# First feed-forward layer: VectorE's operands moved to PSUM, GpSimd's work kept to SBUF

## The chip, the cores and the metric

One core of one Trainium2 chip runs the whole program. The metric is the device time of one execution in microseconds (us). TensorE (PE) multiplies matrices out of SBUF into PSUM; VectorE (DVE), ScalarE (ACT) and GpSimd (POOL) do the elementwise work; SyncE (SP) issues the DMAs. In this program POOL takes operands from SBUF alone; DVE and ACT read SBUF and PSUM.

## The reference

Causal block attention, then two feed-forward layers over the 2304 tokens, with 512 model and 2048 hidden columns. The first layer is the one that the change touches:

```
x = attention(q, k, v)                       # 4 batches, 8 heads, 576 positions, 64 per head
h = x @ w_in                                 # layer 1
g = h * clip(h + 3, 0, 6) / 6
x = g @ w_out
h = x @ w_in2                                # layer 2
g = h * tanh(softplus(h))
out = g @ w_out2
```

Everything is float32, and the kernel keeps that precision by splitting each factor of a product into a high part (rounded to PE's fp32r format) and a low part (the value minus its high part), and adding three products: high by high, high by low, low by high.

## The kernel before

**Stages.** Attention fills the first 205 us of the profiled execution, layer 1 runs to about 575 us, layer 2 to the end. Layer 1 works on five blocks of tokens, four of 512 and one of 256. For each block j and each of 16 slices f of 128 hidden columns there is one step n = 16 j + f: `in1(n)` (12 matmuls, 4 pieces of the model columns by 3 products) puts h into one of two PSUM banks, `h0` and `h1` in turn; `activate1(n)` makes g from it; `out1(n)` (12 matmuls) adds g @ w_out into the four PSUM banks `y0` to `y3`. PE's order is written out in `sequence()`: in1(n), out1(n-2), in1(n+1), out1(n-1), and so on. So in1(n+2), which writes the bank of in1(n) again, begins three sets of 12 matmuls after in1(n) has ended. After a block's last step the four y banks are copied out (`o`) by ACT or DVE, and the next block's first out1 writes them again.

**One step's elementwise work** (`activate1`): ACT writes e = relu(h + 3); DVE writes e = min(e, 6) * h, which is 6 g (L985); ACT writes its high part gh; POOL subtracts, gl = e - gh (L873). Buffers e, gh and gl have three copies each.

**Weights of layer 1** arrive as raw 64-bit words, as two halves c of 512 columns (c = 0 is w_in's, c = 1 w_out's). `rebase` turns a half into float32 in four instructions: ACT writes the scaled high word to a PSUM bank, `r0` or `r1`; POOL writes the sign to an SBUF buffer (`val` or `q`, in turn by f); DVE ORs the shifted low word into that buffer (L895: two SBUF operands); DVE ORs the shifted PSUM bank into it (L899). Then ACT writes the high part `wh` (L922), and POOL, or for c = 1 POOL or DVE, the low part `wl` (L925). `first_weights` does that for f = 4 to 15 while block 0 runs; the earlier ones are made during attention and are not touched.

**Weights of layer 2** are prepared in layer 1 too, by 16 calls of `unit2`, from block 1 on: each rebases two halves, makes four sums `S` of 256 columns, high parts (`hx`, `Sh`, by ACT) and low parts, and stores all to HBM (`w2d`). The two rebased halves go to `q` and `val`, one pair of buffers for even units and one for odd units.

**Tokens** of blocks 1 to 4 (`tokens1`): loads of two halves and a scale, an add on POOL, a multiply by the scale on DVE (L1003), high part on ACT, low part (`xl`, `X`) on DVE or POOL.

**What sets the order.** `Schedule` takes these operations with their dependences, engines and costs, runs a list scheduler over them and issues them in that order, so every engine's queue is fixed when the program is built. Where an operation may run on either of two engines (`either`), it chooses. Kinds in `SHARED` (DVE with SBUF operands alone, POOL) are counted as slower while the other engine works; the kind DVE_PSUM is not. A DMA is counted as landing 2.5 us after its issue.

## Time and profile before

| | |
|---|---|
| median of 3 runs (lowest to highest) | 971.47 us (971.42 to 972.88) |
| profiled execution: its own time / its span | 971.55 us / 969.8 us |
| PE, DVE, ACT, POOL busy, share of the span | 97%, 71%, 54%, 70% |

The span goes from the first to the last instruction of the trace. The profiled execution's own time is 1.75 us longer than its span and 0.08 us above the median. Matmuls overlap one another, so that "97% busy" counts a waiting PE as busy in part. How far PE runs at its full pace is better read from how many matmuls a stretch holds.

### The profile page before, as it was taken

What the parts mean: (1) busy time and instruction counts of PE and PEld (TensorE: products, weight loads), DVE (VectorE), ACT (ScalarE), POOL (GpSimd) and SP (SyncE); (2) the same over time, 40 slices, a digit from 0 to 9 for tenths busy, and PEclk for the clock granted to TensorE, in tenths of its full rate; (3) what the DMA queues carried; (4) which work ended last, traced back from release to release, by engine and by line L of the source; (5) the groups of instructions that cost most, each with busy time, mean ns of one, the idle gap of its engine ahead of it and who ended that gap; (6) DMA issues with size and microseconds to landing.
All of it is one profiled execution on the core that took longest, in us unless ns stands there. A gap on an engine that the chain in (4) does not pass through costs nothing.

```text
span 969.8 us, 16014 instructions
## 1 busy us (share of the span) xinstructions
PE 942.8 (97%) x5300; PEld 857.6 (88%) x5300; DVE 687.8 (71%) x1125; ACT 524.7 (54%) x1241; POOL 678.4 (70%) x663
## 2 busy tenths in 40 slices
PE   8999999999999999999999999999999999999998
PEld 6888889878777877788778899999999999999998
DVE  6798887889899777967841125466689766886567
ACT  4888888865555355445522244554464554744443
POOL 7455554569999789968842237477788877967775
PEclk9999999999999999999999999999999999999999
DMA  5777776799138988788830015867779877787752
GB/s 166 186 198 199 199 180 181 230 297 390 58 99 256 300 272 281 264 283 291 283 123 1 0 45 184 282 237 263 260 242 339 292 252 265 260 293 272 260 192 102
DMA packets 131427, 212.87 MB, mean 220 GB/s; under 512 B 45841, under 2 KB 72465, under 8 KB 131345
## 3 DMA queue, kind: packets, MB, share of 16 engines
q1 hardware_dynamic: 131344, 211.86, 66.8%
q8 instruction: 41, 0.67, 0.3%
q14 instruction: 42, 0.34, 0.1%
HBM read 154.66 MB, written 48.31 MB: 209 GB/s over the span
## 4 chain that ended last, share of the span: by engine, by line
PE 49%; DVE 2%; POOL 2%; DMA 1%; issue 1%; SPq 0%; ACT 0%; POOLq 0%; DVEq 0%
PE y L879 8%; PE y L881 8%; PE y L880 8%; PE h L881 5%; PE h L880 5%; PE h L879 5%; PE r L881 3%; PE r L880 3%; PE r L879 3%; DMA w2d<-hx 1%; POOL gl L873 1%; DMA Sh<-x2d 0%; DVE e L985 0%; DVE S L1026 0%; POOL S L1026 0%
## 5 line engine op out<-in xcount | busy, mean ns | idle before, releaser
L873 POOL TENSOR_TENSOR gl<-e,gh 128x512 fp32r<-128x512 f32 (+1 forms) x79 | 105.8, 1340 | 90.0 <-ACT gh L870 78.9
L879 PE MATMUL y<-gh,wh 128*128 128x512 f32 (+1 forms) x320 | 118.7, 371 | 4.1 <-DVE o L966 3.2
L880 PE MATMUL y<-gl,wh 128*128 128x512 f32 (+1 forms) x320 | 118.4, 370 | 0.0
L881 PE MATMUL y<-gh,wl 128*128 128x512 f32 (+1 forms) x320 | 118.4, 370 | 0.0
L985 DVE SCALAR_TENSOR_TENSOR e<-e,h 128x512 f32<-128x512 f32 (+1 forms) x78 | 48.8, 626 | 81.1 <-ACT e L870 81.1
L1185 DVE TENSOR_TENSOR sgh<-y,sgh 128x384 f32<-128x384 f32 x129 | 69.9, 554 | 32.3 <-PE y L881 32.1
L657 DVE TENSOR_TENSOR t<-t,t 128x512 fp32r<-128x512 f32 (+2 forms) x144 | 69.8, 521 | 23.8 <-ACT t L652 23.6
L870 ACT ACTIVATE gh<-e 128x512 fp32r<-128x512 f32 (+1 forms) x78 | 45.7, 586 | 70.3 <-DVE e L985 70.0
L606 ACT ACTIVATE p<-s,nm 128x64 f32<-128x64 f32 (+2 forms) x144 | 75.0, 529 | 11.9 <-DVE nm L595 11.8
L870 ACT ACTIVATE e<-h 128x512 f32<-128x512 f32 (+1 forms) x78 | 42.5, 544 | 70.4 <-PE h L881 64.1
L879 PEld LDWEIGHTS y<-gh,wh 128*128 128x128 f32 x320 | 60.5, 189 | 15.7 <-ACT o L968 2.7
L880 PEld LDWEIGHTS y<-gl,wh 128*128 128x128 f32 x320 | 60.6, 189 | 10.6 <-POOL gl L873 0.6
L881 PEld LDWEIGHTS y<-gh,wl 128*128 128x128 f32 x320 | 60.6, 189 | 10.1
L881 PE MATMUL h<-xh,wl 128*128 128x512 f32 (+1 forms) x176 | 65.6, 373 | 2.6 <-POOL wl L925 2.6
L880 PE MATMUL h<-xl,wh 128*128 128x512 f32 (+1 forms) x176 | 65.5, 372 | 2.5 <-DVE xl L873 2.5
L676 PEld LDWEIGHTS o<-t,vh 128*128 128x128 f32 x448 | 65.0, 189 | 3.1 <-ACT x L686 0.9
L646 PE MATMUL t<-ident,p 128*128 128x128 f32 x400 | 63.8, 282 | 3.2 <-DVE t L657 3.0
L595 DVE TENSOR_REDUCE nm<-s 128x1 f32<-128x64 f32 (+2 forms) x144 | 63.2, 476 | 5.1 <-PE s L575 5.1
L879 PE MATMUL h<-xh,wh 128*128 128x512 f32 (+1 forms) x176 | 65.4, 372 | 0.3 <-DVE e L985 0.3
L676 PE MATMUL o<-t,vh 128*128 128x320 f32 (+3 forms) x448 | 63.8, 282 | 0.8 <-ACT x L689 0.6
L879 PE MATMUL y<-xh,wh 128*128 128x384 f32 x192 | 64.2, 334 | 0.2 <-issue 0.2
L880 PE MATMUL y<-xl,wh 128*128 128x384 f32 x192 | 64.1, 334 | 0.0
(198 smaller groups left out, 3069.5 us busy)
## 6 DMA issues: line engine op xcount, KB each, us to landing
raw<-w SPq DMA_DIRECT2D x64, 512.0 KB
wh<-w2d SPq DMA_DIRECT2D x48, 512.0 KB
wl<-w2d SPq DMA_DIRECT2D x48, 512.0 KB
wh<-w2d SPq DMA_DIRECT2D x48, 384.0 KB
wl<-w2d SPq DMA_DIRECT2D x48, 384.0 KB
x1d<-x SPq DMA_DIRECT2D x64, 144.0 KB
qb<-qs SPq DMA_DIRECT2D x30, 288.0 KB
w2d<-Sh SPq DMA_DIRECT2D x32, 256.0 KB
```

The lines of the kernel that those rows point to most:

```text
L595: nc.vector.tensor_reduce(nm[:, c:c + 1], sc, axis=AX.X, op=ALU.max, negate=True)
L606: nc.scalar.activation(t, sc, AF.Exp, bias=nm[:, c:c + 1], accum_out=su[:, i:i + 1])
L646: nc.tensor.transpose(tp[:, c, :], t[:, o:o + P], ident)
L657: nc.vector.tensor_sub(z[:, 1, loc, :], tp, f32(z[:, 0, loc, :]))
L676: nc.tensor.matmul(out, lhsT, g[:, t, m0:m1, l, hs], start=(c == t == 0), stop=last and t == 1)
L870: lambda e: nc.scalar.activation(dst, src, func, **kw), after=after)
L873: return plan.add(engines, reads, writes, lambda e: ENG[e].tensor_sub(dst, a, b), **kw)
L879: nc.tensor.matmul(b, wh, xh, start=start and k == 0, stop=False, skip_group_check=True)
L880: nc.tensor.matmul(b, wh, xl, start=False, stop=False, skip_group_check=True)
L881: nc.tensor.matmul(b, wl, xh, start=False, stop=last, skip_group_check=True)
L985: lambda _: nc.vector.scalar_tensor_tensor(e, e, 6.0, h, op0=ALU.min, op1=ALU.mult))
L1185: nc.vector.tensor_add(place(to), bank(b), place(at))
```

## The change

- **`rebase`** now builds the value in the PSUM bank: POOL's sign goes to a scratch buffer; DVE shifts the bank and ORs the sign into it, in place (PSUM and SBUF operands); DVE then ORs the shifted low word (SBUF) with the bank, and writes to the bank itself for c = 0, or to the SBUF buffer for c = 1 (`VAL`). The count of instructions is as before.
- **`first_weights`**: the half c = 0 stays in PSUM bank r0, from which ACT makes wh and DVE (always) wl. The half c = 1 is as before, with wl on either engine.
- **`activate1`**, from block 1 on: DVE writes 6 g over h in its PSUM bank, ACT makes gh from there, and DVE, no longer POOL, makes gl. Block 0 is as before.
- **`tokens1`**: the multiply and the low part are on POOL, except for block 1, where either engine may do both.
- **`unit2`**: the first rebased half is always in r0, the second always in `val1`; there are no longer two pairs in turn. Sums that read r0 are on DVE, the one that doesn't is on POOL. The low parts of `hx` go to `q0` (DVE) and `q1` (POOL) and are stored from there; those of `S` are on POOL.

```diff
--- before.py
+++ after.py
@@ -855,6 +855,7 @@
             buf["X", n, h] = xt[0, 0, n][h] if n < KT else xp.tile(
                 [P, 512], F32R, tag=f"x{'hl'[h]}", name=f"X{n}_{h}")
+    VAL = 1
     W = lambda f, h: weight_tiles(0, f)[h]
     one = lambda e, kind, n: ((e, cost(kind, n), kind in SHARED),)
     either = lambda n: one("DVE", "DVE", n) + one("POOL", "POOL", n)
@@ -880,24 +881,28 @@
             nc.tensor.matmul(b, wh, xl, start=False, stop=False, skip_group_check=True)
             nc.tensor.matmul(b, wl, xh, start=False, stop=last, skip_group_check=True)
-    def rebase(raw, place, val, r, v):
-        high = raw[:, :, 1].bitcast(F32)
-        to, t = buf["r", place], ("r", place)
-        copy(512, [r], [t], to, high, scale=REBASE)
+    def rebase(raw, r, s, names, val=None):
+        high, low = raw[:, :, 1].bitcast(F32), raw[:, :, 0]
+        rn, t, sn, vn = names
+        ids = [len(plan.ops) + n for n in range(4)]
+        copy(512, [rn], [t], r, high, scale=REBASE)
         plan.add(
-            one("POOL", "POOL_ONE", 512), [r], [v], lambda e: nc.gpsimd.tensor_scalar(
-                val, high, 0.0, 1.0, op0=ALU.mult, op1=ALU.mult))
-        bits = val.bitcast(U32)
-        ids = [len(plan.ops) - 2, len(plan.ops) - 1]
-        ids.append(plan.add(
-            one("DVE", "DVE", 512), [r, v], [v],
+            one("POOL", "POOL_ONE", 512), [rn], [sn], lambda e: nc.gpsimd.tensor_scalar(
+                s, high, 0.0, 1.0, op0=ALU.mult, op1=ALU.mult))
+        bits = r.bitcast(U32)
+        to = bits if val is None else val.bitcast(U32)
+        plan.add(
+            one("DVE", "DVE_PSUM", 512), [t, sn], [t],
             lambda e: nc.vector.scalar_tensor_tensor(
-                bits, raw[:, :, 0], 29, bits, op0=ALU.logical_shift_right, op1=ALU.bitwise_or)))
+                bits, bits, 3, s.bitcast(U32), op0=ALU.logical_shift_left, op1=ALU.bitwise_or))
         plan.add(
-            one("DVE", "DVE_PSUM", 512), [t, v], [v],
+            one("DVE", "DVE_PSUM", 512), [rn, t], [t if val is None else vn],
             lambda e: nc.vector.scalar_tensor_tensor(
-                bits, to.bitcast(U32), 3, bits, op0=ALU.logical_shift_left, op1=ALU.bitwise_or))
+                to, low, 29, bits, op0=ALU.logical_shift_right, op1=ALU.bitwise_or))
         return ids
     def first_weights(f):
@@ -911,17 +916,17 @@
         for c in range(2) if not early else ():
             dma(512, [], [names[c]], raw[c].rearrange("p n t -> p (n t)"),
                 w1[f, :, 512 * c:512 * c + 512].bitcast(U32))
+        tag = ("val", "q")[f % 2]
         for c in range(2):
-            tag = ("val", "q")[f % 2]
-            done += rebase(raw[c], c, buf[tag, c], names[c], (tag, c))
+            done += rebase(
+                raw[c], buf["r", c], buf[tag, c], (names[c], ("r", c), (tag, c), (tag, c)),
+                buf[tag, c] if c == VAL else None)
         for c in range(2):
             cs = slice(512 * c, 512 * c + 512)
-            v = buf[tag, c]
+            v, vn = (buf[tag, c], (tag, c)) if c == VAL else (buf["r", c], ("r", c))
+            copy(512, [vn], [("wt", f, c, 0)], W(f, 0)[:, cs], v, psum=c != VAL, after=done)
             plan.add(
-                one("ACT", "ACT", 512), [(tag, c)], [("wt", f, c, 0)],
-                lambda e, cs=cs, v=v: nc.scalar.activation(W(f, 0)[:, cs], v, AF.Copy), after=done)
-            plan.add(
-                one("POOL", "POOL", 512) if c == 0 else either(512), [(tag, c), ("wt", f, c, 0)],
+                either(512) if c == VAL else one("DVE", "DVE_PSUM", 512), [vn, ("wt", f, c, 0)],
                 [("wt", f, c, 1)], lambda e, cs=cs, v=v: ENG[e].tensor_sub(
                     W(f, 1)[:, cs], v, f32(W(f, 0)[:, cs])), after=done)
@@ -979,13 +984,18 @@
         at = ("h", n % 2), ("e", n % 3), ("gh", n % 3), ("gl", n % 3)
         if "a" in parts:
             copy(w, [at[0]], [at[1]], e, h, AF.Relu, True, bias=3.0)
+        if n < FT:
+            g, gn = e, at[1]
+        else:
+            g, gn = h, at[0]
         if "c" in parts:
             plan.add(
-                one("DVE", "DVE_PSUM", w), [at[0], at[1]], [at[1]],
-                lambda _: nc.vector.scalar_tensor_tensor(e, e, 6.0, h, op0=ALU.min, op1=ALU.mult))
+                one("DVE", "DVE_PSUM", w), [at[0], at[1]], [gn],
+                lambda _: nc.vector.scalar_tensor_tensor(g, e, 6.0, h, op0=ALU.min, op1=ALU.mult))
         if "g" in parts:
-            copy(w, [at[1]], [at[2]], gh, e)
-        sub(one("POOL", "POOL", w), [at[1], at[2]], [at[3]], gl, e, f32(gh))
+            copy(w, [gn], [at[2]], gh, g, psum=n >= FT)
+        sub(one("POOL", "POOL", w) if n < FT else one("DVE", "DVE_PSUM", w), [gn, at[2]], [at[3]],
+            gl, g, f32(gh))
     def tokens1(j, k):
         t0, w = BLOCKS[j]
@@ -998,49 +1008,59 @@
                 rsd[k, h:h + 1, t0:t0 + w].to_broadcast([64, w]))
         plan.add(
             one("POOL", "POOL", w), [r, l], [r], lambda e: nc.gpsimd.tensor_add(raw, raw, low))
+        of = either(w) if j == 1 else one("POOL", "POOL", w)
         plan.add(
-            one("DVE", "DVE", w), [r, s, ("xn", 0, 0), ("xn", 0, 1)], [r],
-            lambda e: nc.vector.tensor_mul(raw, raw, rs))
+            of, [r, s, ("xn", 0, 0), ("xn", 0, 1)], [r],
+            lambda e: ENG[e].tensor_mul(raw, raw, rs))
         hi, lo = (buf["X", X(j, k), h][:, :w] for h in range(2))
         at = [("X", X(j, k), h) for h in range(2)]
         copy(w, [r], [at[0]], hi, raw)
-        sub(either(w), [r, at[0]], [at[1]], lo, raw, f32(hi))
+        sub(of, [r, at[0]], [at[1]], lo, raw, f32(hi))
     def unit2(u):
         q, c = u // 2, u % 2
-        at = [("q", u % 2), ("val", u % 2)]
+        at = [("r", 0), ("val", 1)]
         vs = [buf[x] for x in at]
         dst = w2d[q, c].rearrange("t p (s c) -> t p s c", c=256)
         for i in range(2):
             raw = buf["raw", i]
             dma(512, [], [("raw", i)], raw.rearrange("p n t -> p (n t)"),
                 w2[2 * q + i, :, 512 * c:512 * c + 512].bitcast(U32))
-            rebase(raw, i, vs[i], ("raw", i), at[i])
+            rebase(
+                raw, buf["r", i], buf["val", i], (("raw", i), ("r", i), ("val", i), ("val", i)),
+                buf["val", i] if i else None)
         cc, ch = buf["S"], buf["Sh"]
         a11, a12, a21, a22 = vs[0][:, 0:256], vs[0][:, 256:512], vs[1][:, 0:256], vs[1][:, 256:512]
-        def sums(n, a, b, reads, add=False):
+        psum = lambda n: one("DVE", "DVE_PSUM", n)
+        pool = lambda n: one("POOL", "POOL", n)
+        def sums(n, a, b, reads, of, add=False):
             plan.add(
-                either(256), reads, [("S", n)],
+                of, reads, [("S", n)],
                 lambda e: (ENG[e].tensor_add if add else ENG[e].tensor_sub)(cc[:, n], a, b))
-        sums(0, a21, a22, [at[1]], True)
-        sums(3, a11, a21, at)
-        sums(1, cc[:, 0], a11, [at[0], ("S", 0)])
-        sums(2, a12, cc[:, 1], [at[0], ("S", 1)])
+        sums(0, a21, a22, [at[1]], pool(256), True)
+        sums(3, a11, a21, at, psum(256))
+        sums(1, cc[:, 0], a11, [at[0], ("S", 0)], psum(256))
+        sums(2, a12, cc[:, 1], [at[0], ("S", 1)], psum(256))
         view = lambda t: t.rearrange("p (s c) -> p s c", c=256)
+        lo = [view(buf["q", n]) for n in range(2)]
         parts = (
-            (512, view(buf["hx", 0]), view(vs[0]), ("hx", 0), [at[0]], slice(0, 4, 3)),
-            (256, view(buf["hx", 1])[:, 0:1], view(vs[1])[:, 1:2], ("hx", 1), [at[1]], slice(6, 7)),
-            (512, ch[:, 0:2], cc[:, 0:2], ("Sh", 0), [("S", 0), ("S", 1)], slice(1, 3)),
-            (512, ch[:, 2:4], cc[:, 2:4], ("Sh", 1), [("S", 2), ("S", 3)], slice(4, 6)),
+            (512, view(buf["hx", 0]), view(vs[0]), ("hx", 0), [at[0]], slice(0, 4, 3), lo[0], [("q", 0)]),
+            (256, view(buf["hx", 1])[:, 0:1], view(vs[1])[:, 1:2], ("hx", 1), [at[1]], slice(6, 7),
+             lo[1][:, 0:1], [("q", 1)]),
+            (512, ch[:, 0:2], cc[:, 0:2], ("Sh", 0), [("S", 0), ("S", 1)], slice(1, 3), None, None),
+            (512, ch[:, 2:4], cc[:, 2:4], ("Sh", 1), [("S", 2), ("S", 3)], slice(4, 6), None, None),
         )
-        for i, (n, x, v, xn, vn, cs) in enumerate(parts):
-            copy(n, vn, [xn], x.bitcast(F32R), v)
+        for i, (n, x, v, xn, vn, cs, to, tn) in enumerate(parts):
+            of = pool(n) if i else psum(n)
+            to, tn = (v, vn) if to is None else (to, tn)
+            copy(n, vn, [xn], x.bitcast(F32R), v, psum=not i)
             dma(n // 2, [xn], [("w2d", q, c, 0, i)], dst[0][:, cs], x)
-            sub(either(n), vn + [xn], vn, v.bitcast(F32R), v, x)
-            dma(n // 2, vn, [("w2d", q, c, 1, i)], dst[1][:, cs], v)
+            sub(of, vn + [xn], tn, to.bitcast(F32R), v, x)
+            dma(n // 2, tn, [("w2d", q, c, 1, i)], dst[1][:, cs], to)
     WSLOTS = {(0, 0): (7, 8), (1, 0): (9, 10), (0, 1): (11, 12), (1, 1): (13, 14)}
```

Two places in the engines' queues show it. On DVE in block 0, between the c3 instructions (6 g) of steps 7 and 9; first before (names: `e` the activation, `h_0_2` and `h_0_3` the two h banks, `r_3255` and `r_3260` the banks r0 and r1, `raw_0` and `raw_1` the two raw halves):

```order
L985 SCALAR_TENSOR_TENSOR e_3208<-e_3208,h_0_3_3228 128x512
L925 TENSOR_TENSOR wl_8_3515<-val_3263,wh_8_3514 128x512
L895 SCALAR_TENSOR_TENSOR q_3262<-raw_1_3298,q_3262 128x512
L895 SCALAR_TENSOR_TENSOR val_3258<-raw_0_3299,val_3258 128x512
L899 SCALAR_TENSOR_TENSOR q_3262<-r_3260,q_3262 128x512
L899 SCALAR_TENSOR_TENSOR val_3258<-r_3255,val_3258 128x512
L895 SCALAR_TENSOR_TENSOR val_3263<-raw_1_3300,val_3263 128x512
L985 SCALAR_TENSOR_TENSOR e_3270<-e_3270,h_0_2_3215 128x512
```

and the same place of DVE's queue with the change:

```order
L994 SCALAR_TENSOR_TENSOR e_3208<-e_3208,h_0_3_3228 128x512
L900 SCALAR_TENSOR_TENSOR r_3260<-r_3260,val_3263 128x512
L930 TENSOR_TENSOR wl_9_3310<-r_3255,wh_9_3309 128x512
L904 SCALAR_TENSOR_TENSOR val_3263<-raw_1_3312,r_3260 128x512
L900 SCALAR_TENSOR_TENSOR r_3255<-r_3255,val_3258 128x512
L904 SCALAR_TENSOR_TENSOR r_3255<-raw_0_3311,r_3255 128x512
L994 SCALAR_TENSOR_TENSOR e_3270<-e_3270,h_0_2_3215 128x512
```

Every row between the two c3 instructions now has one operand in PSUM, and the low part made there is that of the half c = 0. On DVE in block 1, from the c3 of step 26 on (`S`, `Sh`, `hx` belong to a unit of layer 2's weights), before:

```order
L985 SCALAR_TENSOR_TENSOR e_3270<-e_3270,h_0_2_3215 128x512
L899 SCALAR_TENSOR_TENSOR q_3262<-r_3255,q_3262 128x512
L1026 TENSOR_TENSOR S<-S,q_3262 128x256
L1026 TENSOR_TENSOR S<-q_3262,S 128x256
L873 TENSOR_TENSOR S<-S,Sh 128x512
L985 SCALAR_TENSOR_TENSOR e_3193<-e_3193,h_0_3_3228 128x512
L895 SCALAR_TENSOR_TENSOR val_3258<-raw,val_3258 128x512
L899 SCALAR_TENSOR_TENSOR val_3258<-r_3260,val_3258 128x512
```

and with the change:

```order
L994 SCALAR_TENSOR_TENSOR h_0_2_3215<-e_3270,h_0_2_3215 128x512
L874 TENSOR_TENSOR gl_3272<-h_0_2_3215,gh_3271 128x512
L874 TENSOR_TENSOR q_3257<-r_3255,hx_3259 128x512
L900 SCALAR_TENSOR_TENSOR r_3260<-r_3260,val_3263 128x512
L904 SCALAR_TENSOR_TENSOR val_3263<-raw,r_3260 128x512
L994 SCALAR_TENSOR_TENSOR h_0_3_3228<-e_3193,h_0_3_3228 128x512
L900 SCALAR_TENSOR_TENSOR r_3255<-r_3255,val_3258 128x512
L904 SCALAR_TENSOR_TENSOR r_3255<-raw,r_3255 128x512
L874 TENSOR_TENSOR gl_3206<-h_0_3_3228,gh_3200 128x512
L1042 TENSOR_TENSOR S<-S,r_3255 128x256
```

The product is written over h, its low part gl has come to DVE, behind zero to two other instructions, and the subtraction S<-S,Sh has left it for POOL.

## Rows read from the trace of the kernel before

**Rows 1.** The page's busy times: us, share of the span, count of instructions.

```profile
PE 942.8 (97%) x5300; PEld 857.6 (88%) x5300; DVE 687.8 (71%) x1125; ACT 524.7 (54%) x1241; POOL 678.4 (70%) x663
```

**Rows 2.** Stretches, PE alone: from:to, us, busy (matmuls), granted clock, DMA share, GB/s.

```profile
214.34:282.00 67.66, 65.38 (x286) 1.00 0.53 196
282.00:310.00 28.00, 25.55 (x109) 1.00 0.73 235
...
355.00:388.00 33.00, 30.80 (x132) 1.00 0.81 268
388.00:406.00 18.00, 15.93 (x63) 0.91 0.85 282
...
470.00:494.00 24.00, 21.28 (x92) 1.00 0.83 284
```

**Rows 3.** Stretches, all engines: us, then PE, PEld, DVE, ACT, POOL, clock, DMA.

```profile
205.00:290.00 85.00, 82.10 (x360) 66.42 (x359) 77.11 (x83) 47.61 (x86) 80.00 (x65) 1.00 0.57 204
...
205.00:496.00 291.00, 279.27 (x1207) 225.46 (x1206) 240.60 (x274) 148.73 (x272) 250.65 (x213) 0.99 0.76 257
```

**Rows 4.** PE's waits, 205 to 500 us: total us, times, longest us.

```profile
PE y L879 <- DVE o L966: 3.2, 2, 2.1
PE h L881 <- POOL wl L925: 2.6, 3, 1.8
PE h L880 <- DVE xl L873: 2.5, 2, 1.5
PE h L879 <- DVE e L985: 2.0, 4, 0.8
```

**Rows 5.** DVE's groups by shape, 205 to 496 us: count, busy us, mean ns, idle.

```profile
L895 DVE SCALAR_TENSOR_TENSOR val<-raw,val 128x512 uint32<-128x512 uint32 x28 | 35.4, 1263 | 24.2 <-POOL val L889 24.2
L895 DVE SCALAR_TENSOR_TENSOR q<-raw,q 128x512 uint32<-128x512 uint32 x28 | 33.5, 1196 | 2.9 <-POOL q L889 2.9
L985 DVE SCALAR_TENSOR_TENSOR e<-e,h 128x512 f32<-128x512 f32 x49 | 33.1, 676 | 1.2 <-ACT e L870 1.1
L873 DVE TENSOR_TENSOR S<-S,Sh 128x512 fp32r<-128x512 f32 x20 | 23.6, 1187 | 5.4 <-ACT Sh L870 2.8 <-POOL S L1026 2.3
...
L1003 DVE TENSOR_TENSOR xr<-xr,xn 128x512 f32<-128x512 f32 x12 | 15.8, 1313 | 0.0
```

**Rows 6.** POOL's groups by shape, the same stretch and columns.

```profile
L873 POOL TENSOR_TENSOR gl<-e,gh 128x512 fp32r<-128x512 f32 x49 | 75.4, 1538 | 14.5 <-ACT gh L870 13.8 <-DVE q L895 0.5
L889 POOL TENSOR_SCALAR val<-raw 128x512 f32<-128x512 f32 x28 | 22.5, 806 | 2.8 <-DMA w2d<-val 2.0 <-POOL gl L873 0.7
```

**Rows 7.** DVE and POOL in order of time: start us, us, instruction.

```profile
269.29 1.80 DVE L895 SCALAR_TENSOR_TENSOR val<-raw,val 128x512 uint32<-128x512 uint32 x1
...
391.86 0.41 DVE L873 TENSOR_TENSOR val<-val,hx 128x256 fp32r<-128x256 f32 x1
...
270.50 1.71 POOL L925 TENSOR_TENSOR wl<-q,wh 128x512 fp32r<-128x512 f32 x1
272.18 1.28 POOL L873 TENSOR_TENSOR gl<-e,gh 128x512 fp32r<-128x512 f32 x1
```

**Rows 8.** PE in order of time: first matmul of out1(0) and of in1(4).

```profile
214.34 0.39 PE L879 MATMUL y<-gh,wh 128*128 128x512 f32 x1
...
219.78 0.39 PE L879 MATMUL h<-xh,wh 128*128 128x512 f32 x1
```

**Rows 9.** The chain of waits near 438 us: start us, us, what.

```profile
438.24 0.61 DVE e L985
438.87 0.64 ACT gh L870
439.58 0.51 POOL gl L873
```

**Rows 10.** A wait for a store, 205 to 500 us; DVE at block 4's loads.

```profile
ACT hx L870 <- DMA w2d<-hx: 14.3, 15, 4.1
...
487.51 0.43 DVE L1003 TENSOR_TENSOR xr<-xr,xn 128x256 f32<-128x256 f32 x1 [2.13 <-DMA xn<-rsd]
```

## The prediction

> **What bounds the kernel now.** Read the page's busy times first [rows 1]: PE is at 97%, so the end is set by PE's work plus what PE waits. Then ask where it waits. The pace comes from PE's order of time: out1(0) and out1(1), 24 matmuls, take 219.78 - 214.34 = 5.44 us [rows 8], 0.2267 us each, 2.72 us for a set of 12, 5.44 us for a step. A matmul's record, 0.39 us, is 1.7 times that, so a stretch of L us at full pace lists L / 0.2267 + 1.7 matmuls, those cut by its edges among them. The same sum for the slow stretches [rows 2] gives what PE lost: 214 to 282 us holds 286 of 300, 3.2 us; 282 to 310 holds 109 of 125, 3.7; 355 to 388 holds 132 of 147, 3.4; 388 to 406 holds 63 of 81, 4.1; 470 to 494 holds 92 of 107.5, 3.5. Together 17.9 us, all inside layer 1. That is the whole purse; layer 2 keeps PE full.
>
> Who made PE wait [rows 4]: copies of y out of PSUM by DVE at block ends, low parts of weights by POOL, low parts of tokens by DVE, and DVE's product e (the h bank not yet free). Four causes, two engines, so look at those as a whole: from 205 to 290 us DVE is busy 77.1 and POOL 80.0 of 85 us; over the layer 240.6 and 250.7 of 291 us [rows 3]. They are full, and their instructions are long for a reason that the groups show [rows 5]: the shift L895, with two SBUF operands, takes 1263 or 1196 ns on average, while L985, same size, with one operand in PSUM, takes 676 on average over 49 instances, beside the same POOL. In order of time it is plain on both sides [rows 7]: a shift of 1.80 us and a POOL subtraction of 1.71 us lie over each other, and the subtraction at 272.18, of the same shape, takes 1.28. So two SBUF operands on DVE cost 0.5 to 1.1 us for each instruction and 0.4 us for POOL's beside it. [...]
>
> **The change part by part**, against 971.55 us (span 969.8 plus 1.75; the median is 971.47).
>
> *DVE, 205 to 496 us.* The 56 low shifts get a PSUM operand: 35.4 + 33.5 = 68.9 us become 56 x 0.68 = 38.1, a gain of 30.8. The 20 subtractions S<-S,Sh leave: 23.6. Of 12 wide multiplies of tokens 7 leave: 7 x 1.31 = 9.2 [rows 5]. The gl of steps 16 to 49 arrive: 34 x 0.68 = 23.1 more. The other moves (sums of 256 columns, 31 to 48, at 0.41 [rows 7] instead of up to 1.1; low parts from r0 in place of those from SBUF) come out level to within about 6 us. Net -40, DVE at some 200 of 291 us.
>
> *POOL.* 34 gl leave: 34 x 1.54 = 52.3 [rows 6]. S<-S,Sh arrives: 20 x 1.28 = 25.6. The multiplies arrive: 11 of 512 columns and 4 of half that, about 17. Some 7 low parts of weights leave, 7 x 1.7 = 12 [rows 7]. Net -22, before what every remaining instruction saves where DVE no longer lies over it (up to 0.4 us). POOL at 200 to 230.
>
> *Block 0, by step.* DVE had the product, two shifts of 1.23, two ORs with r (one PSUM operand, so 0.68) and one low part of about 1.1: 5.6 us against PE's 5.44, so it fell behind until PE waited. Now 0.68 + 4 x 0.68 + 0.68 = 4.1. POOL: 1.54 + 2 x 0.81 + 1.5 x 1.7 = 5.7, now 1.28 + 2 x 0.81 + 1.28 = 4.2. Both have over 1 us of room in each step. The loop that is now serial, r0 held from ACT's write until wl is made, is an ACT write, two DVE instructions, an ACT copy and a DVE subtraction: 2 x 0.64 + 3 x 0.68 = 3.3 us plus five hand-overs, under 0.1 us each by the chain near 438 us (0.61 + 0.64 of 1.34 [rows 9]); under 4 us of the 5.44. Of the 6.9 us lost between 214 and 310 I keep 1.0 (0.5 for a step in which two chains meet, 0.5 for the block's end).
>
> *Blocks 1 to 3.* The h bank is now held for ACT's e, the product, gh and gl: about 0.65 + 1.34 + 0.68 = 2.7 us (from product to gl 1.34 [rows 9]), and PE wants it after three sets, 8.16 us; 5.5 us of cover. If that cover goes, each us beyond it is a us of PE. Of the 3.4 us between 355 and 388 I keep 0.7. At the block's end the two copies of y on DVE stood behind instructions of 1.4 to 1.8 us and now stand behind 0.7; with no wait of 2 us the clock should not fall either; of 4.1 I keep 1.0.
>
> *The end, 470 to 494 us.* The token low part (longest wait 1.5 [rows 4]) should go; the wait at the block's end has DVE behind a load, 2.13 us for the scale [rows 10], which the change doesn't touch. Of 3.5 I keep 1.8.
>
> *Queues.* SP's bytes are the same; in each unit the stores of S and Sh now stand ahead of those of hx and q, and q is stored from two new buffers. DVE's write to q0 and POOL's to q1 wait for the previous unit's store. ACT already has that wait on hx: 15 times, 14.3 us in all, 4.1 at most [rows 10]. On DVE it lies under the 5.5 us cover, so I take it as 0, with 0 to 20 us as its bounds (below).
>
> *A price that no row has:* DVE writing PSUM, 118 times in place between 214 and 494 us (84 on r, 34 on h). Nearest is 0.68 with PSUM read; below, nothing suggests less, as the shortest rows with SBUF alone are not shorter. Above, reading and writing one bank in turn would add a second pass: 256 columns more take 0.68 - 0.41 = 0.27 [rows 5, 7], so 0.54. I take 0.68.
>
> [...]
>
> **Sum.** Kept: 1.0 + 0.7 + 1.0 + 1.8 = 4.5 us of 17.9; gone: 13.4. 971.5 - 13.4 = 958 us.
>
> **The rivals.**
> *Half only (16%).* Shorter instructions, but the queues are fixed at build time and waits for DMA (raw halves, stores, token loads) hold them at block ends as before; units with one pair of buffers make this likelier. Then the 6.9 us of block 0 go, little else: 964, within 963 to 969.
> *Banks held too long: slower (8%).* Place: DVE's queue in blocks 1 to 3, between the product and gl, where the new q0 write can wait for a store. It decides from 5.5 us of delay beyond the 2.7. Waits of the 4.1 us kind plus a queue of two or three instructions reach that. If each of 16 units cost PE 1.5 us: +24 - 13 = +11, about 982. Against it: the mean of those waits is 1 us. [...]
> *PSUM in place costs a second pass: slower (5%).* Block 0's DVE step becomes 4.1 + 3 x 0.54 = 5.7 us, over 5.44; it decides from about 0.45 more. The layer's DVE time is 200 + 64 = 264, above today's 241, and today's losses come back with 5 us more: 976.
> *It doesn't do what it says (5%).* If the stretching were of any DVE work beside POOL, PSUM operands would not help and times would move within 2 us of 971.5. The 676 ns mean of L985 speaks against it.
>
> **How the numbers follow.** The forecast, 953 to 963, has 66%; half only 16%; no change 5%; slower 13%. The floor is the whole purse gone, 971.5 - 17.9 = 953.6; a us below for what smaller stretches lose: 952.5. The forecast and half only hold 82% between 952.5 and 969. About 0.2%, 2 us, is what a measurement tells from no change: faster than 969.5 has 0.82, the same 0.05, slower 0.13.
>
> **What would show it.** Right: DVE's shifts at 0.68 us, POOL's subtractions at 1.28, DVE busy near 200 of 291 us and POOL under 230, no wait of PE for wl, no stretch with a lower clock, the last matmul of layer 1 some 13 us earlier and layer 2 as long as before. Wrong: in-place instructions near 1.2 us; PE waiting for h with gl as the releaser; DVE idle for stores of q; PE's waits at block ends unchanged.

## The result, and the profile after

The changed kernel takes 954.91 us (median of 5 runs, 954.69 to 955.31) against 971.47 us for the kernel before: a ratio of 0.9826 [0.9808, 0.9845], 16.6 us less. The profiled run took 954.69 us, with a span of 952.9. Forecast were 958 us and a range of 952.5 to 969.

The page's busy times, which answer to [rows 1]:

```profile
PE 936.5 (98%) x5300; PEld 857.8 (90%) x5300; DVE 642.3 (67%) x1173; ACT 524.2 (55%) x1240; POOL 587.2 (62%) x616
```

The same five stretches of PE as in [rows 2] (from:to, us, busy (matmuls), granted clock, DMA share, GB/s):

```profile
214.34:282.00 67.66, 67.66 (x301) 1.00 0.67 236
282.00:310.00 28.00, 28.00 (x125) 1.00 0.93 296
355.00:388.00 33.00, 33.00 (x147) 1.00 0.87 302
388.00:406.00 18.00, 18.00 (x81) 1.00 0.91 293
470.00:494.00 24.00, 24.00 (x108) 1.00 0.14 50
```

They hold 301, 125, 147, 81 and 108 matmuls, the counts of full pace, where before had 286, 109, 132, 63 and 92. The clock of 0.91 is gone too. PE's one wait between 205 and 500 us (total, times, longest) is at the end of attention; none is left in layer 1, so nothing answers to [rows 4]:

```profile
PE o L676 <- ACT x L689: 0.7, 1, 0.7
```

Layer 1 from its first matmul on y to layer 2's first on r, in order of time on PE (start us, us, instruction); before's first y is in [rows 8], its first r is the first row here, and the other two are of after:

```profile
615.76 0.34 PE L879 MATMUL r<-wh,wh 128*128 128x384 f32 x1
```

```profile
215.56 0.39 PE L880 MATMUL y<-gh,wh 128*128 128x512 f32 x1
...
598.55 0.34 PE L880 MATMUL r<-wh,wh 128*128 128x384 f32 x1
```

Before it is 615.76 - 214.34 = 401.42 us, after 598.55 - 215.56 = 382.99: 18.43 us less. The rest of the span is level: from r on 969.8 - 615.76 = 354.0 us before, 952.9 - 598.55 = 354.3 after. After's first y is 1.2 us later, in a part that the change doesn't touch.

All engines, as in [rows 3] (us, then PE, PEld, DVE, ACT, POOL, clock, DMA):

```profile
205.00:290.00 85.00, 84.74 (x378) 70.41 (x379) 64.58 (x95) 54.69 (x99) 75.53 (x72) 1.00 0.72 250
205.00:496.00 291.00, 290.74 (x1287) 240.98 (x1288) 189.16 (x301) 153.59 (x280) 191.23 (x195) 1.00 0.76 258
```

DVE fell from 240.6 to 189.2 us with 27 instructions more (301 against 274), POOL from 250.7 to 191.2 with 18 fewer. The groups of DVE in that stretch, as in [rows 5]:

```profile
L900 DVE SCALAR_TENSOR_TENSOR r<-r,val 128x512 uint32<-128x512 uint32 x44 | 30.5, 696 | 14.3 <-POOL val L894 10.6 <-ACT r L871 3.2
L994 DVE SCALAR_TENSOR_TENSOR h<-e,h 128x512 f32<-128x512 f32 x38 | 26.3, 693 | 42.4 <-ACT e L871 42.2
L874 DVE TENSOR_TENSOR gl<-h,gh 128x512 fp32r<-128x512 f32 x38 | 26.1, 687 | 8.4 <-ACT gh L871 8.2
L904 DVE SCALAR_TENSOR_TENSOR r<-raw,r 128x512 uint32<-128x512 uint32 x28 | 19.4, 694 | 0.8
L904 DVE SCALAR_TENSOR_TENSOR val<-raw,r 128x512 uint32<-128x512 uint32 x22 | 15.1, 685 | 0.5
```

and of POOL, as in [rows 6]:

```profile
L874 POOL TENSOR_TENSOR S<-S,Sh 128x512 fp32r<-128x512 f32 x32 | 41.6, 1308 | 32.9 <-ACT Sh L871 24.8 <-DVE S L1042 5.5 <-ACT hx L871 2.6
L894 POOL TENSOR_SCALAR val<-raw 128x512 f32<-128x512 f32 x44 | 28.9, 662 | 12.6 <-DMA raw<-w 11.5
L874 POOL TENSOR_TENSOR gl<-e,gh 128x512 fp32r<-128x512 f32 x15 | 19.4, 1296 | 4.2 <-ACT gh L871 3.6 <-ACT gh L413 0.6
```

The low shifts are at 0.69 us (1.26 and 1.20 before), POOL's subtractions at 1.30 (1.54), its sign instruction at 0.66 for 44 of the 56 (0.81; the other 12, into `q`, took 0.77). What can't be read from this pair is which part of the change paid for which part of the 18.4 us. The experiments are about that.

### The profile page after: what moved, and what is told of

Its sections match the earlier page's. It is cut to its first block, busy times and chain, and to the rows that moved or that the text cites. A ratio compares the mean times of both kernels' runs of the same rounds, so it can differ in the third digit from the quotient of the medians.

```text
span 952.9 us, 15987 instructions
## 1 busy us (share of the span) xinstructions
PE 936.5 (98%) x5300; PEld 857.8 (90%) x5300; DVE 642.3 (67%) x1173; ACT 524.2 (55%) x1240; POOL 587.2 (62%) x616
## 4 chain that ended last, share of the span: by engine, by line
PE 88%; DVE 5%; ACT 3%; DMA 2%; issue 1%; POOL 0%; SPq 0%; ACTq 0%; DVEq 0%; POOLq 0%
PE y L881 13%; PE y L882 13%; PE y L880 13%; PE h L881 10%; PE h L882 10%; PE h L880 10%; PE o L676 3%; PE r L882 3%; PE r L881 3%; PE r L880 3%; PE t L646 2%; ACT p L606 2%; PE s L573 2%; DVE nm L595 1%; PE s L574 1%; PE s L575 1%
## 5 line engine op out<-in xcount | busy, mean ns | idle before, releaser
L994 DVE SCALAR_TENSOR_TENSOR h<-e,h 128x512 f32<-128x512 f32 (+1 forms) x64 | 40.2, 627 | 97.0 <-ACT e L871 96.8
L882 PE MATMUL y<-xh,wl 128*128 128x384 f32 x192 | 64.1, 334 | 0.0
L880 PE MATMUL h<-wh,wh 128*128 128x384 f32 x192 | 64.1, 334 | 0.0
```

The lines of the kernel that those rows point to most:

```text
L880: nc.tensor.matmul(b, wh, xh, start=start and k == 0, stop=False, skip_group_check=True)
L882: nc.tensor.matmul(b, wl, xh, start=False, stop=last, skip_group_check=True)
L994: lambda _: nc.vector.scalar_tensor_tensor(g, e, 6.0, h, op0=ALU.min, op1=ALU.mult))
```

## The experiments

Every run stands beside runs of the kernel before on the same chip, whose medians there were 972.3 to 973.4 us; the ratio goes by those. PE's loss is read as in the prediction, by the matmuls of a stretch at 0.2267 us each, in two stretches: 216.5 to 312 us (block 0 and its end; full pace is 423) and 312 to 500 us (blocks 1 to 3 as far as the weights of layer 2 are made; full pace is 831). The losses are those of one profiled run each, and the runs of one kernel lie up to 6.7 us apart (e3, e11), so small differences between losses say little. Every edit also has the whole schedule built anew, so the order of the queues changes with it.

| kernel | us, median | ratio to before | lost to 312 us | lost 312 to 500 us |
|---|---|---|---|---|
| before | 971.47 | | 393: 6.8 us | 780: 11.6 us |
| after | 954.91 | 0.9826 | 423: 0 | 831: 0 |
| e1: low shift on SBUF | 963.81 | 0.9899 [0.988, 0.9917] | 384: 8.8 | 830: 0.2 |
| e2: gl on SBUF | 954.87 | 0.9806 [0.9785, 0.9827] | 423: 0 | 831: 0 |
| e3: shifts alone | 963.46 | 0.9883 [0.9857, 0.991] | 423: 0 | 777: 12.2 |
| e4: product alone | 967.32 | 0.9931 [0.991, 0.9951] | 391: 7.3 | 812: 4.3 |
| e5: gl three times | 955.81 | 0.983 [0.98, 0.9859] | 423: 0 | 826: 1.1 |
| e6: gl five times | 967.36 | 0.9937 [0.9913, 0.9961] | 423: 0 | 826: 1.1 |
| e7: product undone | 954.84 | 0.9811 [0.9786, 0.9836] | 423: 0 | 831: 0 |
| e8: tokens undone | 955.21 | 0.9815 [0.9786, 0.9844] | 423: 0 | 831: 0 |
| e9: shifts and units | 954.61 | 0.9826 [0.9795, 0.9858] | 423: 0 | 824: 1.6 |
| e10: units undone | 955.61 | 0.983 [0.9805, 0.9856] | 423: 0 | 831: 0 |
| e11: shifts, low parts on POOL | 960.02 | 0.988 [0.9836, 0.9924] | 423: 0 | 802: 6.6 |
| e12: units alone | 970.61 | 0.9973 [0.9956, 0.999] | 395: 6.3 | 782: 11.1 |

The first theory is the prediction's: two SBUF operands on DVE beside POOL make both engines slow and full, and PE's waits follow from that in the whole layer. The rival for each part is that it is not needed.

**e1, the low shift with two SBUF operands again, all else as after.** In `rebase` the shifted low word is ORed into the sign buffer first, as before, and the PSUM bank comes second:

```diff
-                bits, bits, 3, s.bitcast(U32), op0=ALU.logical_shift_left, op1=ALU.bitwise_or))
+                sb, low, 29, sb, op0=ALU.logical_shift_right, op1=ALU.bitwise_or))
...
-                to, low, 29, bits, op0=ALU.logical_shift_right, op1=ALU.bitwise_or))
+                to, bits, 3, sb, op0=ALU.logical_shift_left, op1=ALU.bitwise_or))
```

(`sb` is the sign buffer, `bits` the bank.) Two things come with this edit. The order of the two ORs is swapped, and the scheduler still counts the shift as DVE_PSUM, that is as not slowed by POOL.

> The changed kernel with one thing undone: the low shift takes two SBUF operands again (sign buffer and raw word, into the sign buffer), and the second shift ORs the PSUM bank with it and writes where the changed kernel writes. Same count of instructions on each engine. Theory C (two SBUF operands on DVE beside POOL stretch both): the low shifts go from 0.69 to 1.0 to 1.2 us, DVE gains about 20 us of busy time between 205 and 496 us, POOL's instructions beside them lengthen by up to 0.4 us, PE waits for low parts of weights in block 0 again; 957 to 962 us. Theory M (the gain came from moving work between the engines and from a plan that fits, wherever the operands lie): 954 to 956 us.

Measured: 963.81 us, dearer than either theory. The shift's group in e1 (DVE, 205 to 496 us), and PE's two rows at the end of block 0 with the wait in brackets, then that stretch with its clock:

```profile
L900 DVE SCALAR_TENSOR_TENSOR val<-raw,val 128x512 uint32<-128x512 uint32 x44 | 46.3, 1062 | 22.7 <-POOL val L894 22.7
```

```profile
305.14 0.77 PE L880 MATMUL y<-gh,wh 128*128 128x512 f32 x1 [2.69 <-ACT o L973]
305.70 0.63 PE L881 MATMUL y<-gl,wh 128*128 128x512 f32 x1
```

```profile
304.00:312.00 8.00, 6.86 (x18) 5.40 (x19) 4.27 (x7) 4.83 (x10) 7.68 (x7) 0.57 0.84 280
```

One operand in SBUF instead of PSUM takes the shift from 0.69 to 1.06 us, and block 0 loses 8.8 us: waits of which the last is 2.69 us for the copy of y, and then a stretch with a mean granted clock of 0.57. There 15 matmuls take 6.37 us (305.14 to 311.51) instead of 3.40, 0.425 us each instead of 0.2267, so about 3 of the 8.8 us are the clock's; in the kernel before the clock stayed at 1.00 in block 0. After 312 us 0.2 us are lost. So the shift's form (its operand, and with it the order of the two ORs) decides block 0, and with the other parts in place it isn't needed later.

**e2, gl from two SBUF operands on DVE.** The product goes to `e` as before, gl stays on DVE:

```diff
-            g, gn = h, at[0]
+            g, gn = e, at[1]
```

> The changed kernel with the product g in SBUF (e) again: DVE writes it over e, gh is made from e, and DVE still makes gl, now from two SBUF operands. POOL's and SP's queues are the same, the h banks are free two instructions earlier. Theory C: gl goes from 0.69 to about 1.0 us on average (POOL is busy two thirds of that stretch), 34 of them, some 10 us of DVE time; POOL's subtractions from 1.31 to 1.45; blocks 1 to 3 have room for it, so 954.5 to 957 us. Theory M: gl stays at 0.69. If the long hold of the h banks cost anything now hidden, the time would fall below 954.5.

Measured: 954.87 us, and this group:

```profile
L874 DVE TENSOR_TENSOR gl<-e,gh 128x512 fp32r<-128x512 f32 x38 | 34.9, 919 | 8.6 <-ACT gh L871 8.2
```

The stretch is there (0.92 us against 0.69) and costs nothing: PE has no wait left to lengthen. Writing the product over h isn't what brought the gain.

**e3, before with the shifts alone changed**, both values going to SBUF as before:

```diff
-                bits, raw[:, :, 0], 29, bits, op0=ALU.logical_shift_right, op1=ALU.bitwise_or)))
+                pb, pb, 3, bits, op0=ALU.logical_shift_left, op1=ALU.bitwise_or))
...
-                bits, to.bitcast(U32), 3, bits, op0=ALU.logical_shift_left, op1=ALU.bitwise_or))
+                bits, raw[:, :, 0], 29, pb, op0=ALU.logical_shift_right, op1=ALU.bitwise_or)))
```

> The kernel before with one thing of the change: the sign is ORed into the PSUM bank first and the low shift then takes one SBUF operand and the bank, for both halves into the SBUF buffers as before; nothing moves between engines. Theory C: 56 shifts from 1.23 to 0.69 us, 30 us less on DVE, the 6.9 us that PE lost from 214 to 310 us mostly gone and part of the rest; 958 to 965 us. Theory M: 969 to 971.5 us.

(`pb` is the PSUM bank, `bits` the SBUF buffer.) Measured: 963.46 us; the profiled run is the longest of its four, 967.24. The second stretch, all engines:

```profile
312.00:500.00 188.00, 180.62 (x777) 144.11 (x776) 130.89 (x169) 89.69 (x165) 137.68 (x129) 1.00 0.80 265
```

Block 0 is mended whole, and 312 to 500 us loses 12.2, no less than before's 11.6, though DVE is busy 130.9 us there instead of 142.6. The other runs of e3 are shorter: its median is 9.9 us below before's, 3 us more than block 0's 6.8, so on average the shifts give back perhaps 3 us from block 1 on, and most of the loss there stays. What DVE does ahead of PE's first matmul of an in1 at 423.15 us, which comes 0.2 us late for e, in order of time:

```profile
419.24 1.57 DVE L873 TENSOR_TENSOR q<-q,hx 128x512 fp32r<-128x512 f32 x1
420.73 1.77 DVE L873 TENSOR_TENSOR S<-S,Sh 128x512 fp32r<-128x512 f32 x1
422.43 0.67 DVE L985 SCALAR_TENSOR_TENSOR e<-e,h 128x512 f32<-128x512 f32 x1
```

The product stands behind two instructions of a unit of layer 2's weights, both with two SBUF operands, 3.3 us together. That gave the next theory: the units, and not the shifts, are what loses PE's time from block 1 on. But this place costs PE only 0.2 us, and at dearer ones something else stands ahead. The longest wait for e (0.86 us) comes after DVE stood idle for 7.70 us until POOL's sign came, and POOL for 3.05 of these until a store of `val` had landed:

```profile
328.57 0.66 POOL L889 TENSOR_SCALAR val<-raw 128x512 f32<-128x512 f32 x1 [3.05 <-DMA w2d<-val]
329.26 0.70 DVE L895 SCALAR_TENSOR_TENSOR r<-r,val 128x512 uint32<-128x512 uint32 x1 [7.70 <-POOL val L889]
331.34 0.50 PE L879 MATMUL h<-X,wh 128*128 128x512 f32 x1 [0.86 <-DVE e L985]
```

The wait of 1.71 us for a copy of y comes after DVE waited 1.54 us for a load, and the instruction that had waited then took 1.41 us, ahead of the copy at 485.82 us:

```profile
484.49 1.41 DVE L873 TENSOR_TENSOR val<-Sh,q 128x384 f32<-128x384 f32 x1 [1.54 <-DMA Sh<-x2d]
486.64 0.47 PE L879 MATMUL y<-gh,wh 128*128 128x512 f32 x1 [1.71 <-DVE o L966]
```

The longest of all, 2.07 us for xl at 473.30, does follow long instructions on DVE: 1.51 us for a sum S, then 1.75 us for xl itself.

**e4, before with the product alone moved** (over h from block 1 on, gl on DVE): the change's lines in `activate1` and no others.

```diff
+            g, gn = h, at[0]
...
-        sub(one("POOL", "POOL", w), [at[1], at[2]], [at[3]], gl, e, f32(gh))
+        sub(one("POOL", "POOL", w) if n < FT else one("DVE", "DVE_PSUM", w), [gn, at[2]], [at[3]],
+            gl, g, f32(gh))
```

> The kernel before with one thing of the change: from block 1 on the product is written over h in PSUM and DVE makes gl from there; shifts, tokens and units as before. Theory C: POOL loses 52 us, DVE gains 23 us beside shifts that still take 1.2 us, so DVE becomes the fuller engine in blocks 1 to 3 while block 0 is unchanged; 964 to 974 us. Theory M: the losses of blocks 1 to 3 (11 us) go, block 0's stay; 960 to 964 us.

Measured: 967.32 us; block 0 loses as before, 312 to 500 us 4.3 instead of 11.6. PE's waits for two causes (total, times, longest):

```profile
PE h L879 <- DVE gl L873: 2.7, 5, 0.8
PE h L881 <- POOL wl L925: 2.6, 3, 1.8
```

The second row is that of [rows 4], in block 0. The first is new: with DVE still as full as before (238.0 of 291 us), PE does wait for the h bank with gl as the releaser, five times, 0.8 us at most. That is the prediction's rival of the banks, in small.

**e5 and e6, after with gl done three and five times over** on DVE from block 1 on (same operands, same result); e6 has 5 in place of 3:

```diff
+        for _ in range(1 if n < FT else 3):
             sub(one("POOL", "POOL", w) if n < FT else one("DVE", "DVE_PSUM", w), [gn, at[2]], [at[3]],
                 gl, g, f32(gh))
```

> The kernel after, with DVE's subtraction gl done three times over from block 1 on instead of once (same operands, same result): two more DVE instructions of about 0.69 us in each step, nothing else. It adds 38 x 2 x 0.69 = 52 us to DVE between 290 and 496 us (124.6 of 206 us after, so about 177; before it was 163.5 there) and 1.4 us to the hold of the h bank (2.7 to 4.1 us of 8.16). Theory 'cover' (a step on DVE shorter than 5.44 us and a hold shorter than 8.16 us cost PE nothing, and before's losses came from long instructions beside POOL, not from the load of DVE as such): 955 to 958 us, waits of PE in layer 1 under 3 us. Rival 'load' (any DVE as full as before's loses what before lost from 310 us on): 961 to 968 us, with waits for o and xl or gl at block ends.

> As the run with gl three times, but five times over: four more DVE instructions in each step from block 1 on. 38 x 4 x 0.69 = 105 us more, so DVE would need 124.6 + 105 = 230 us where layer 1's steps give it 206. Both theories expect DVE to become the bound: 'cover' 975 to 990 us (24 us more than DVE has, plus its waits for ACT that it can no longer make up), PE waiting for h with gl as the releaser. Were the time under 965 us, DVE would have had more room than the busy times show, and the sum by busy time would be wrong.

Measured: 955.81 and 967.36 us. The stretch from 312 us in e5, and then in e6:

```profile
312.00:500.00 188.00, 187.78 (x826) 154.40 (x825) 156.25 (x256) 88.66 (x163) 97.75 (x106) 1.00 0.78 254
```

```profile
312.00:500.00 188.00, 187.10 (x826) 154.57 (x825) 179.76 (x287) 78.97 (x141) 74.10 (x81) 1.00 0.54 180
```

With DVE at 156 of 188 us, more than before's 142.6, PE loses 1.1 us: DVE's load as such is not what cost before its time. The h bank is held 1.4 and 2.8 us longer, which costs 1.1 us at most in this stretch. In e6 the expectation failed in size and place: the time is 967, not 975 to 990, and most of the loss comes later. DVE is 96% busy, so the order that was fixed at build time puts the units off (POOL falls to 74 us and the DMA share to 0.54). The last S<-S,Sh starts at 596.9 us, where after's started at 453.6 (min/median/max, first and last start, in e6):

```profile
L874 POOL TENSOR_TENSOR S<-S,Sh x32: 1272/1297/1312, 285.4 to 596.9; 128x512 fp32r<-128x512 f32 x32
```

The loss comes in layer 1's last block, of 256 tokens, from 560 to 600 us, where after has 329 matmuls and no wait. There the expected cause is found, PE waiting for h with gl as the releaser (e6's stretch, then its wait in it: total, times, longest):

```profile
560.00:600.00 40.00, 34.72 (x269) 33.28 (x268) 34.56 (x85) 16.10 (x37) 12.93 (x14) 0.98 0.50 175
```

```profile
PE h L880 <- DVE gl L874: 5.3, 4, 2.0
```

**e7, the product undone** in after (SBUF, gl on POOL), and **e8, the tokens undone** (multiply on DVE, low part on either engine). In e7, and then in e8:

```diff
-        sub(one("POOL", "POOL", w) if n < FT else one("DVE", "DVE_PSUM", w), [gn, at[2]], [at[3]],
-            gl, g, f32(gh))
+        sub(one("POOL", "POOL", w), [at[1], at[2]], [at[3]], gl, e, f32(gh))
```

```diff
-        of = either(w) if j == 1 else one("POOL", "POOL", w)
+        of = either(w)
...
-            of, [r, s, ("xn", 0, 0), ("xn", 0, 1)], [r],
+            one("DVE", "DVE", w), [r, s, ("xn", 0, 0), ("xn", 0, 1)], [r],
```

> The kernel after, with the product in SBUF and gl on POOL again, as before; shifts, tokens and units stay changed. DVE loses 26 us (189 to about 163 in 205 to 496 us), POOL gains 34 to 38 x 1.3 to 1.5 = 44 to 57 us (191 to 235 to 248). Theory 'needed' (the product's move is what lets the token work and S<-S,Sh go to POOL; without it POOL is as full as before): 958 to 964 us, waits of PE for gl or xl in blocks 1 to 3. Rival 'padding' (with the shifts shortened there is room enough for POOL to keep gl): 954 to 957 us and no waits.

> The kernel after, with the tokens as before: the multiply by the scale on DVE, the low part on either engine. 7 wide multiplies go back to DVE at 1.1 to 1.3 us (8 to 9 us), POOL loses as much. Theory 'room' (with the shifts and the product changed, the place of the token work no longer decides): 954 to 957 us, PE's waits in layer 1 under 1.5 us. Rival 'tokens' (the waits for xl and o that remain with the shifts alone, 2.24 us at 473 and 1.87 us at 487, come from this work on DVE): 957 to 961 us, with those two waits back.

Measured: 954.84 and 955.21 us, no loss in either stretch. For e7 the theory that the move is needed falls: POOL is as full as I had put it, 236.8 of 291 us, and PE waits for nothing. Each of the two parts, product and tokens, can be undone by itself where the rest of the change stays.

**e9, shifts and units without product and tokens** (e7 and e8 together), and **e10, after with the units as before**, their shifts in the new form:

```diff
-        at = [("r", 0), ("val", 1)]
+        at = [("q", u % 2), ("val", u % 2)]
...
-            sub(of, vn + [xn], tn, to.bitcast(F32R), v, x)
+            sub(either(n), vn + [xn], vn, v.bitcast(F32R), v, x)
```

> The kernel after, with both the product (gl on POOL, in SBUF) and the tokens as before: what is left of the change is the shifts, the half c = 0 of block 0 in r0, and the units (their low parts on POOL or with r0 as an operand). It is the run of the shifts alone plus those. Theory 'units' (the 11.8 us of PE's waits that remained with the shifts alone come from DVE standing behind the units' instructions with two SBUF operands, S<-S,Sh at 1.12 us on average and 1.77 at most, q<-q,hx at 1.2): 954 to 957 us, waits of PE in layer 1 under 2 us. Rival 'either of two' (product or tokens must have moved too, the runs that undo one of them lean on the other): 958 to 963 us, waits for xl and e left.

> The kernel after, with the units as before (both rebased halves go to SBUF, two pairs of buffers, sums and low parts on either engine, no separate q); only their shifts keep the new form. Product and tokens stay changed. Theory 'units': what the units do on DVE with two SBUF operands comes back (S<-S,Sh, q<-q,hx, about 24 us), DVE about 205 to 220 of 291, waits of PE of 3 us and more, 958 to 964 us. Rival 'room' (POOL is 45 us emptier than with the shifts alone, so that the scheduler gives it the low parts, and any two of the three parts do): 954 to 957 us.

Measured: 954.61 and 955.61 us, with 1.6 and 0 us lost after 312 (e9's profiled run is the longest of its four, 957.90). So the units suffice beside the shifts, as the theory said, but they aren't necessary: product and tokens do the same without them, as the rival said. No single part is the cure for blocks 1 to 3.

**e11, the shifts alone (e3) with the units' low parts all on POOL:**

```diff
-            sub(either(n), vn + [xn], vn, v.bitcast(F32R), v, x)
+            sub(one("POOL", "POOL", n), vn + [xn], vn, v.bitcast(F32R), v, x)
```

> The run of the shifts alone with one word changed: all low parts of the units are on POOL, instead of on either engine. 33 instructions of 0.95 to 1.2 us leave DVE (S<-S,Sh x17, q x6, val x10: 35.6 us of its 213), POOL gets them at 1.3 and 0.74 (some 37 us on 234, so 255 to 270 with less stretching). Theory 'DVE stands behind long instructions': waits for e and o go, 956 to 961 us. Rival 'POOL full' (POOL at about 265 of 291 becomes what is late): 962 to 970 us, PE's waits for gl and xl grow.

Measured: 960.02 us. The profiled run loses about half of what e3's lost after 312 us (6.6 of 12.2), but against before on the same chip the two kernels are equal (ratios 0.988 and 0.9883, and their runs overlap: 957.6 to 964.3 and 960.6 to 967.2 us). So it is not shown that taking the long instructions off DVE helps. PE's waits for e have nearly gone (one, 0.2 us), its waits for copies of y have not (2.3 us), and POOL is at 160.7 of 188 us:

```profile
312.00:500.00 188.00, 184.77 (x802) 150.81 (x802) 109.93 (x149) 88.45 (x162) 160.68 (x153) 0.99 0.78 263
```

**e12, the units alone**: e9 with e1's edit, so that the low shift has two SBUF operands. The edits are the three shown at e7, e8 and e1, and as in e1 the scheduler counts the shift as DVE_PSUM, so the order is built on too short a price.

> The run with shifts and units (product and tokens as before), with the low shift on two SBUF operands again, so that the part without the shifts' new operands is left: units, half c = 0 in r0. Theory 'two stages' (the low shift's two SBUF operands are what block 0 loses by, 6.5 to 8.6 us between 214 and 312 us; blocks 1 to 3 lose by the load that units or the product take away, not by the shift's form): 962 to 966 us, 6 to 9 us lost before 312 us, under 3 after it. Rival 'the shift in all blocks' (the shorter shifts are needed beside the units from block 1 on as well): 967 to 972 us, 5 us or more lost after 312 us.

Measured: 970.61 us. Block 0 loses 6.3, as both theories had it, and 312 to 500 us loses 11.1: the time is the rival's, and "from block 1 on only the load counts" falls. All engines, and DVE in order of time ahead of PE's wait of 0.79 us for e at 375.99 us:

```profile
312.00:500.00 188.00, 182.04 (x782) 146.44 (x781) 108.32 (x163) 87.54 (x161) 135.93 (x129) 0.99 0.80 264
```

```profile
369.45 0.69 DVE L874 TENSOR_TENSOR q<-r,hx 128x512 fp32r<-128x512 f32 x1 [2.35 <-ACT hx L871]
370.06 1.85 DVE L900 SCALAR_TENSOR_TENSOR val<-raw,val 128x512 uint32<-128x512 uint32 x1
371.94 0.69 DVE L904 SCALAR_TENSOR_TENSOR val<-r,val 128x512 uint32<-128x512 uint32 x1
372.55 0.68 DVE L900 SCALAR_TENSOR_TENSOR val<-raw,val 128x512 uint32<-128x512 uint32 x1
...
375.26 0.68 DVE L990 SCALAR_TENSOR_TENSOR e<-e,h 128x512 f32<-128x512 f32 x1
```

DVE waits 2.35 us for hx (ACT, which makes hx, had itself waited 2.39 us for a store of `hx`) with the product eight places behind in its queue. The first shift then takes 1.85 us beside a POOL subtraction from 370.07 to 371.37 us. The one at 372.55 takes 0.68: it started 0.17 us ahead of POOL, and POOL's sum of 256 columns beside it took 1.12 us instead of the 0.74 that it takes on average in after. But the longest wait of PE in this stretch, 1.84 us for X at 386.42 us, comes 5.7 us behind a place where DVE stood idle for 4.74 us until the store of `q` had landed:

```profile
380.68 0.69 DVE L874 TENSOR_TENSOR q<-r,hx 128x512 fp32r<-128x512 f32 x1 [4.74 <-DMA w2d<-q]
```

Two more waits for e (0.58 us at 457.97, 0.57 at 469.83) come after DVE idled for 4.76 us (for hx) and 4.21 us (for the store of `q`), with shifts of 0.68 us in between. So in e12 stores that hold DVE's queue stand ahead of PE's waits as well as long shifts, and what part each has isn't shown.

**What the runs say together.** Block 0: the low shift's form, and none of the other parts. Every kernel with the short shift loses 0 there, every one without it (before, e1, e4, e12) 6.3 to 8.8 us. Blocks 1 to 3: each of three parts alone leaves a loss (shifts 12.2, units 11.1, product 4.3 us), and every two of them that were run take it away (shifts and units 1.6; shifts, product and tokens 0; product, units and tokens 0.2; no run has a pair with the product and without the tokens). **Left open** is what measure orders these. The sum of DVE's and POOL's busy time between 312 and 500 us does not: e12 has 108.3 + 135.9 = 244 us and loses 11.1, e5 has 156.3 + 97.8 = 254 and loses 1.1. The rows of e3 and e12 show two things ahead of what PE waits for in a queue of fixed order: long instructions, and DVE standing idle for a store, a load or POOL's sign. How much each costs isn't shown; a run that changes the order alone, or takes the stores away, wasn't made.

## Why the prediction was right, step by step

**The purse.** Right. The loss was put at 17.9 us, all in layer 1; layer 1 became 18.43 us shorter and has no wait left.

**What I kept.** This is the term that was mis-sized: of the 4.5 us kept, 0 was left. That is more than the difference between 958 and 954.9 (3.1 us), as layer 1 began 1.2 us later. 1.0 for meeting chains in block 0 and 1.7 for blocks 1 and 2 were guesses, and nothing of the kind appears. The 1.0 that was left of the 4.1 us between 388 and 406 us also took it that the clock falls with a wait of 2 us. No run shows a wait from which it falls: e3's stayed at 1.00 after 2.07 us. What before's trace shows there is a wait of 2.07 us too, and 1.2 us later nine matmuls in 3.64 us instead of 2.04 (399.67 to 403.31 us) at a mean granted clock of 0.53, so 1.6 of the 4.1 us; after has neither in that stretch (before's wait, then its slow matmuls):

```profile
398.44 0.47 PE L879 MATMUL y<-gh,wh 128*128 128x512 f32 x1 [2.07 <-DVE o L966]
```

```profile
399.67:403.31 3.64, 3.64 (x10) 0.53 0.72 227
```

The 1.8 at the end rested on DVE waiting behind a load ([rows 10], 2.13 us). The multiply is now on POOL, and that wait with it:

```profile
POOL xr L1014 <- DMA xn<-rsd: 3.4, 3, 1.5
```

What stands behind it are tokens of block 4, whose first matmul comes at 547.4 us. I had said that the change doesn't touch that wait; it moved the instruction that waits. I had also passed over a second load, nearer to the copy of y at 489.83 us. A wait for such a load is still on DVE after the change and costs nothing: the copy runs at 469.79 us, and PE waits for none (before, then after):

```profile
489.35 0.56 DVE L873 TENSOR_TENSOR raw<-Sh,raw 128x384 f32<-128x384 f32 x1 [1.41 <-DMA Sh<-x2d]
```

```profile
465.02 0.56 DVE L874 TENSOR_TENSOR val<-Sh,q 128x384 f32<-128x384 f32 x1 [2.13 <-DMA Sh<-x2d]
```

**DVE, net -40 to about 200 us.** Measured -51.4, to 189.2. Two named terms hold: 56 low shifts at 0.69 make 38.6 us (38.1 forecast), gl 26.1 (38 in the stretch where I had 34: 23.1). The multiplies were mis-counted: I let 7 wide ones leave (9.2 us), while my own sum for POOL had 11 wide and 4 half ones arrive; those left, 18.0 us by their groups. "The other moves level to within 6 us" was wrong too: token low parts went to POOL (9.7 us by their groups), and sums with two SBUF operands (0.72 to 1.09 us for 256 columns) became instructions of 0.42 us or went to POOL, 48 for 20.2 us where 31 had taken 26.8.

**POOL, net -22, 200 to 230 us.** Measured -59.4, to 191.2, below the range. I set the saving by less stretching aside ("before what every remaining instruction saves") and gave it only a range. By the groups of both traces, what stayed on POOL became some 25 us shorter in all (an estimate: count times the fall of the mean; the sign instructions from 0.81 to 0.66 and 0.77 us, gl from 1.54 to 1.30). The rest I had left out: of the units' work sums and a low part that went to DVE took some 27 us off POOL, and token low parts brought some 9.

**Block 0 by step.** Right in the outcome: block 0 loses nothing, and e1 and e3 show that the shift's form is the cause. DVE's 64.6 of 85 us is 4.1 of each 5.44, the forecast number, but in part by luck: it is an average over steps with and without weights, and the same average was 4.9 before, where my sum had 5.6. POOL has 75.5 of 85, 4.8 of 5.44 where I had 4.2; I had left out the token work of block 1 that runs there.

**Blocks 1 to 3.** The outcome was right, the reason only half. The sum took the shorter shifts (-30.8 us) as the largest relief for the whole layer. From block 1 on they give back little by themselves (e3: 12.2 us lost in the profiled run, by the median perhaps 3 us gained), and aren't needed beside the others (e1). The forecast held because the change has three remedies where two suffice, which I didn't know; so far it was luck. Thinking engine by engine over 291 us hid that; the stages had to be asked one at a time.

**The bank and its cover.** Right for this change: no wait of PE for gl. e6 holds h for 2.8 us more and loses 1.1 us to 500 us; only in the last block, with DVE full, does PE wait 5.3 us for h. The store wait that I took as 0, with 20 us as its upper bound, did come, and lay under the cover (total, times, longest):

```profile
DVE q L874 <- DMA w2d<-q: 13.6, 9, 2.8
ACT hx L871 <- DMA w2d<-hx: 6.4, 9, 1.9
```

ACT's wait fell from 14.3 us to 6.4, so together they are 20.0 us where one was 14.3. In e12, where the shifts are long, one such wait lasts 4.74 us and stands ahead of a wait of PE. e5 shows room for a longer hold in this kernel (1.4 us more, and one wait for gl, of 0.2 us), and e4 and e6 show the other side: with a full DVE the hold costs PE 2.7 and 5.3 us.

**In place in PSUM.** Taken at 0.68 us, measured at 0.693 to 0.696; a second pass of 0.54 us would have made it 1.22, so that rival falls. Between 0.676 for the product before (PSUM read, SBUF written) and 0.696 in place after lie 0.02 us; after's subtractions of 512 columns with one operand in PSUM take 0.685 to 0.689.

**The rivals.** "Half only" put 964 us. The whole change did better, but e3, with the shorter shifts alone, ends there with 963.5, and in part for the reason given (waits for DMA): its waits at 331.34 and 486.64 us follow a store and a load. The longest, at 473.30, follows long instructions. That the change doesn't do what it says is out, since every shift shortened.

## What to carry to other kernels

Split the loss by stage and ask for each stage which part of a change reaches it: here the form of one shift settled block 0, and for the later blocks three remedies overlapped, so that their single gains (shifts none to 3 us, units 0.5, product 7.3, of 11.6, mostly by one profiled run each) say little of what they give together. In queues that are fixed at build time, look at what stands ahead of the instruction that PE waits for before you add up busy time: it may be a long instruction, or one that itself waits for a store or for another engine. When two engines that stretch each other are relieved (here DVE's low shift from 1.26 to 0.69 us, POOL's gl from 1.54 to 1.30), count the shortening of what stays, on both.
